# A new order table for a fused attention and adapter kernel on one core

## The chip, the core and the metric

The kernel runs on one NeuronCore of a Trainium2 chip. TensorE (PE) does the matmuls and their weight loads, VectorE (DVE) and ScalarE (ACT) turn what stands in PSUM into bf16 tiles in SBUF, GpSimd (POOL) only issues loads, and SyncE (SP) issues stores and transposing transfers. The metric is device microseconds of one launch. A span runs from the first to the last instruction of one profiled execution.

## The reference

Relu-squared attention over 8 batches of 12 heads, 448 positions and 64 columns, and after it a mixture of two out of eight rank-16 adapters on the 3584 x 768 result:

```python
def _attn_ref(q, k, v):
    scores = q.shape[-1] ** -0.5 * np.matmul(q, k.transpose(0, 1, 3, 2))
    attn = np.maximum(scores, 0.0) ** 2 / S
    return np.matmul(attn, v)

def _moe_ref(x, w_gate, A, B):
    logits = x @ w_gate
    topk = np.argpartition(-logits, 2, axis=1)[:, :2]
    w = softmax(logits at topk)
    ...
    delta[mask] += w[mask, k, None] * ((x[mask] @ A[e]) @ B[e])
    return x + delta
```

## The kernel before

`build` makes a list of some 1,100 operations, each a short run of instructions for one engine, and `ordered` puts them in the order of the string `ORDER`, which also gives each its PSUM banks (`@4`) and, where two engines can do it, its engine (`:A` for ACT, `:D` for DVE). Nothing else orders the work: each engine runs its instructions strictly in the order of the table and waits on semaphores for what an instruction reads or overwrites. The durations that operations carry (`act`, `dve`, 0.81 and so on) are for a planner outside and do not run on the chip.

A tile is one of 24 pairs (b, q) of batch and quad of four heads. Its names are:

- `f` with a number: operations without a key, above all the loads of q, k and v, two DMAs each, from POOL (`load`, L185). Buffers: five q, five k, eight v. They are named `q_5_1` for tile (5, 1). `f24` is the load of B (L248).
- `tp`, `te`: transposes of q and k on PE (L313), and their copy to the tile `qT` on DVE (L327, L335).
- `qk` n, `relu` n, `sq` n, `pv` n: for n from 0 to 173, one block of scores on PE (four 64x64 matmuls, L452), its relu out of PSUM on ACT (L472) or DVE (L474) into the tile `a`, the square of two or three blocks on DVE (L489), and the product with v (L520). There are eleven `a` buffers. A number of `relu` is used as a clock in what follows: "at relu 100" means where that word stands in the table.
- `x`: the result of seven `pv`, cast into `xt` by ACT or DVE (L565).
- `z`, `gmax` to `gzp`, `zt`, `zT`: gate and adapter input of a group of three 128-row tiles: PE (L582), small DVE and ACT steps, PE transposes (L644), and the copy `zT` by ACT or DVE (L661).
- `b`, `o`, `st`: half an output tile on PE, three transposes of `xt` (L728) and an fp32 product with B in two passes (L737); its copy out of PSUM by ACT or DVE (L773) or, for tiles 15 to 23, its sum with a transposed `xt` on DVE (L764); the store from SP or ACT (L783). For tiles 15 to 23 `xb` are transposing DMAs on SP (L677).
- `f86` is a run of eight matmuls on zeros (L348); `f84`, `f85`, `f87` are the first transposes and `f88` to `f91` their copies.

The gate's product leaves, per row, 128 adapter columns and then 8 logits, side by side in PSUM; `aw` builds the weights for that (L258).

Of the kernel before, what the change touches and what calls it, by code (L numbers as in the profile page):

```python
# [14 lines left out]
J = 7  # L15
CUT = 3
SPIN = 8
PH = 64
QUADS = 3
NB = 8  # L20
S = J * PH
# [12 lines left out]
C = dict(late=6, xi=(), om=(), merge_x=0, sqp=((999, (2, 2, 3)),), om2=(), fl=(), gf=(), ai=4, tg=((15, 3), (18, 3), (21, 3)), sp=(), xbdur=1.45, bx=8, xh=2, apart=3, apcap=1, gl=(3, 1), tqlat=2.0)  # L34
# [5 lines left out]
f4 f3 f1 f0 f2 f6 f5 f8 f7 f11 f9 f10 f84@0 f12 f88 f85@2 f90 f89 f13 f87@4 qk0@6 f91 qk1@0 relu0:D qk2@2 f14  # L40
relu1:A qk3@4 relu2:D relu3:A tp2@6 f17 qk4@0 te2 relu4:A qk5@2 qk6@4 sq2 tp3@6 f16 relu5:A f86@0 te3 relu6:A
sq0 qk7@0 f15 qk8@2 qk9@6 relu7:A tp4@4 relu8:D relu9:A f18 qk10@0 te4 qk11@2 relu10:A qk12@6 sq4 tp5@4 f19
relu11:A qk13@0 relu12:A te5 tp6@2 f26 sq9 relu13:A qk14@4 qk15@6 tp7 relu14:A f23 sq7 pv0@0 pv1 pv2 relu15:A
pv3 qk16@4 te6 pv4 pv5 f20 relu16:A pv6 qk17@6 x13:D pv7@2 relu17:A qk18@4 sq11 f22 pv8 pv9 x12:A qk19@6
relu18:A pv10 qk20@0 relu19:D f21 pv11 relu20:A pv12 pv13 qk21@4 sq16 x27:A qk22@6 f27 qk23@0 relu21:A aw1@3
sq14 relu22:A f33 x26:D relu23:A qk24@4 tp8@6 ae1 f25 relu24:A sq18 qk25@0 qk26@2 tp9 relu25:A f55 pv14@4 pv15
pv16 te8 relu26:A pv17 qk27@0 f31 pv18 pv19 relu27:A pv20 sq23 qk28@2 qk29@6 x41:A f28 qk30@0 x40:D relu28:A
aw0@5 sq25 relu29:A f29 relu30:A qk31@2 ae0 tp10@6 tp11 f32 relu31:A sq21 qk32@4 qk33@0 relu32:A te10 pv21@2 f30
pv22 pv23 relu33:A qk34@4 sq30 qk35@6 relu34:A qk36@0 f37 relu35:D relu36:A qk37@4 pv24 pv25 relu37:A pv26 sq32
f35 qk38@6 tp12@0 pv27 relu38:A tp13 qk39@4 f43 x55:A te12 qk40@6 x54:A z0@3 relu39:A sq35 qk41@0 f34 z1  # L50
relu40:A qk42@4 relu41:D z2 relu42:A f38 qk43@6 gmax0 tp14@0 relu43:A sq28 qk44@4 tp15 f42 relu44:A gd0 qk45@6
gu0 te14 relu45:A qk46@4 f50 gt0 sq39 qk47@0 relu46:A pv28@6 pv29 pv30 gsg0 pv31 f24 relu47:A qk48@4 pv32 gw0
pv33 sq44 f48 pv34 relu48:A qk49@0 gzp0 x69:A f36 tp18@4 sq37 relu49:A tp19 pv35@2 zt0@7 zt1 zt2 x68:A f41 te18
qk50@0 zT0:A pv36 pv37 relu50:A qk51@6 sq46 pv38 pv39 f47 relu51:A pv40 qk52@4 qk53@0 pv41 relu52:A x82:D tp16@6
tp17 relu53:A te16 qk54@4 b2@2 relu54:A f44 sq49 qk55@0 o2:A qk56@6 qk57@4 relu55:A relu56:D b0@2 f49 x83:A
relu57:D qk58@0 o0:A qk59@6 f39 relu58:A z3@3 z4 sq51 relu59:A qk60@4 qk61@0 z5 f40 sq56 relu60:A b4@2 relu61:A
gmax3 qk62@6 f46 sq58 b1@4 relu62:A gu3 gd3 qk63@0 o4:A gt3 f65 sq42 qk64@6 gsg3 o1:A b3@5 relu63:A gw3 gzp3
b5@2 f51 relu64:A sq60 zt3@4 zt4 o3:A zt5 pv42@0 o5:A pv43 st2 qk65@6 zT3:A sq53 pv44 pv45 relu65:A qk66@2 st4
pv46 pv47 pv48 relu66:A tp20@4 st0 qk67@6 x96:D tp21 x97:A te20 f53 pv49@2 relu67:A pv50 qk68@0 pv51 pv52 sq63
relu68:A pv53 f66 pv54 pv55 qk69@4 qk70@6 x110:A relu69:D qk71@0 relu70:A f45 b6@2 x111:D relu71:A qk72@4 o6:D  # L60
tp22@6 relu72:A sq65 qk73@0 tp23 pv56@2 relu73:A pv57 f74 qk74@4 te22 pv58 pv59 relu74:A pv60 qk75@0 f79 pv61
sq67 pv62 relu75:A qk76@6 b8@4 f64 relu76:A x124:D qk77@0 x125:A sq70 tp24@6 relu77:A tp25 qk78@2 f59 z6@5 te24
relu78:A qk79@0 z7 relu79:A f52 o8:D qk80@2 qk81@6 sq72 z8 relu80:A b10@4 f54 gmax6 relu81:A sq77 qk82@0 tp26@2
# [81 lines left out]
def build(k=None, c=C):  # L145
# [31 lines left out]
    def load(b, w, q, deps):  # L177
        nm = "qkv"[w]

        def fn():  # L180
# [7 lines left out]
        o = op(("POOL",), 1.17, fn, deps=deps, kind="load", take=(nm, "lane"), give=("lane",))  # L188
        o.mb = 1.35
        return o  # L190

# [763 lines left out]
```

## Time and profile before

| | us |
|---|---|
| median of 3 runs (181.57 to 182.73) | 181.69 |
| span of the profiled execution | 179.6 |
| PE busy | 165.1 |
| DVE busy | 163.5 |
| ACT busy | 156.2 |
| POOL busy | 90.7 |

The profiled execution's own time is not recorded beside its span; the median run stands 2.1 us above the span. An engine's busy time is the union of its instructions' spans, and instructions that follow each other on one engine overlap in these spans by some 0.1 to 0.2 us, so the pace of an engine is read from start to start, not from the mean duration. A busy PE is not PE at its peak.

In a timeline each row is: start, duration, engine, line, operation, output <- input, how many instructions are merged, and in brackets the idle time before and what ended it. In a table of stretches each row is: from and to, length, busy time of PE, PEld (weight loads), DVE, ACT and POOL with instruction counts, the granted clock as a share of 2.4 GHz, the DMA share and GB/s.

### The profile page before, as it was taken

How to read it: one execution, taken by the hardware profiler on the slowest of the kernel's cores; microseconds unless marked ns; L12 is line 12 of the kernel's file. 1: busy time of each engine (PE TensorE's matmuls, PEld its weight loads, DVE VectorE, ACT ScalarE, POOL GpSimd, SP SyncE). 2: the span in 40 equal slices, each digit the busy share in tenths (PEclk: the TensorE clock that was granted, in tenths of full speed). 3: DMA queues.
4: the chain of work that ended last, by engine and by line, in shares of the span. 5: the costliest groups of instructions: out<-in, count | busy, mean ns of one | idle time of the engine just before them, and what ended most of it. 6: DMA issues, size and time to landing. Idle time of an engine off the chain costs nothing.

```text
span 179.6 us, 7694 instructions
## 1 busy us (share of the span) xinstructions
PE 165.1 (92%) x3366; PEld 99.2 (55%) x3366; DVE 163.5 (91%) x254; ACT 156.2 (87%) x240; POOL 90.7 (50%) x155
## 2 busy tenths in 40 slices
PE   7887998888899999999979899999999999999990
PEld 2445476454535665646646465655666557576650
DVE  0699999999989999999999899999999999999831
ACT  3399999999999999999998999999999899993120
POOL 7999997988869377850966867250000000000000
PEclk9999999999999999999999999999999999999999
DMA  4999999999999999994699999988495663515644
GB/s 90 126 170 188 164 112 183 164 180 178 202 180 152 186 303 166 175 166 130 84 176 299 197 185 268 237 118 222 113 171 149 45 223 63 189 42 211 230 194 158
DMA packets 33985, 30.49 MB, mean 170 GB/s; under 512 B 11488, under 2 KB 30432, under 8 KB 33952
## 3 DMA queue, kind: packets, MB, share of 16 engines
q0 software_dynamic: 22000, 17.03, 65.7%
q1 hardware_dynamic: 11376, 11.90, 22.1%
q10 hardware_dynamic: 576, 1.08, 1.6%
q8 instruction: 26, 0.43, 0.9%
q14 instruction: 7, 0.06, 0.1%
HBM read 33.84 MB, written 11.01 MB: 250 GB/s over the span
## 4 chain that ended last, share of the span: by engine, by line
PE 44%; ACT 16%; DMA 16%; POOL 15%; issue 4%; DVE 2%; ACTq 0%; POOLq 0%
PE ps L737 17%; ACT a L472 14%; DMA q<-in_q_dram 9%; PE ps L452 9%; PE ps L520 8%; POOL k L185 5%; PE ps L582 4%; POOL v L185 4%; DMA B<-in_moe_B_dram 4%; POOL q L185 3%; PE ps L728 3%; DMA k<-in_k_dram 3%; PE ps L313 2%; ACT osb L773 2%; PE ps L644 1%
## 5 line engine op out<-in xcount | busy, mean ns | idle before, releaser
L472 ACT ACTIVATE a<-ps 128x896 bf16<-128x896 f32 (+3 forms) x158 | 132.7, 961 | 3.3 <-PE ps L452 3.0
L489 DVE TENSOR_TENSOR a<-a 128x1792 bf16<-128x1792 bf16 (+4 forms) x75 | 88.5, 1193 | 0.0
L452 PE MATMUL ps<-qT 64*64 64x448 bf16 (+2 forms) x756 | 57.9, 345 | 4.5 <-ACT a L472 3.3
L737 PE MATMUL ps<-B,zT 128*128 128x384 f32 x112 | 47.5, 514 | 0.3 <-DMA B<-in_moe_B_dram 0.3
L520 PE MATMUL ps<-a,v 64*64 64x448 bf16 (+2 forms) x756 | 44.3, 330 | 0.8 <-ACT a L472 0.4
L452 PEld LDWEIGHTS <-qT 64*64 64x64 bf16 x756 | 25.3, 106 | 31.9 <-issue 22.9
L185 POOL DMA_DIRECT2D k<-in_k_dram x46 | 27.8, 629 | 16.3 <-PE ps L452 7.1
L185 POOL DMA_DIRECT2D v<-in_v_dram x48 | 28.8, 621 | 8.1 <-PE ps L452 3.8
L185 POOL DMA_DIRECT2D q<-in_q_dram x48 | 29.4, 639 | 3.5 <-DMA v<-in_v_dram 1.5
L520 PEld LDWEIGHTS <-v 64*64 64x64 bf16 x756 | 22.6, 106 | 7.9 <-issue 2.7
L327 DVE COPY qT<-ps 128x1792 bf16<-128x1792 bf16 x21 | 22.8, 1084 | 0.7 <-ACT a L472 0.4
L565 ACT CAST xt<-ps 128x448 bf16<-128x448 f32 (+2 forms) x37 | 19.4, 560 | 2.6 <-PE ps L520 2.3
L773 ACT COPY osb<-ps 128x384 f32<-128x384 f32 x26 | 13.1, 529 | 7.4 <-PE ps L737 5.6
L737 PEld LDWEIGHTS ps<-B,zT 128*128 128x128 f32 x112 | 17.3, 190 | 3.7 <-DMA B<-in_moe_B_dram 0.4
L474 DVE TENSOR_SCALAR a<-ps 128x896 bf16<-128x896 f32 (+1 forms) x16 | 16.9, 1069 | 0.9 <-PE ps L452 0.9
L313 PEld LDWEIGHTS <-q 64*64 64x64 bf16 x672 | 10.4, 112 | 6.9 <-issue 3.3
L582 PEld LDWEIGHTS <-xt 128*128 128x128 bf16 x168 | 10.5, 98 | 5.7 <-issue 4.7
L582 PE MATMUL ps<-awg,xt 128*128 128x136 bf16 x168 | 13.5, 223 | 0.0
L728 PEld LDWEIGHTS <-xt 128*128 128x128 bf16 x114 | 8.0, 98 | 9.9 <-issue 8.1
L313 PE MATMUL ps<-identb,q 64*64 64x64 bf16 x672 | 10.9, 197 | 2.3 <-DMA q<-in_q_dram 1.1
L728 PE MATMUL ps<-identb,xt 128*128 128x128 bf16 x114 | 12.7, 220 | 0.2
L565 DVE CAST xt<-ps 128x448 bf16<-128x448 f32 (+2 forms) x17 | 9.6, 570 | 0.2 <-PE ps L520 0.2
(47 smaller groups left out, 97.9 us busy)
## 6 DMA issues: line engine op xcount, KB each, us to landing
out_dram<-osb SPq DMA_DIRECT2D x25, 384.0 KB, 4.2
q<-in_q_dram POOLq DMA_DIRECT2D x48, 112.0 KB, 5.0
v<-in_v_dram POOLq DMA_DIRECT2D x48, 112.0 KB, 4.9
k<-in_k_dram POOLq DMA_DIRECT2D x46, 112.0 KB, 4.9
out_dram<-osb ACTq DMA_DIRECT2D x2, 384.0 KB, 2.3
B<-in_moe_B_dram POOLq DMA_DIRECT2D x1, 384.0 KB, 6.6
xb<-xt SPq DMA_TRANSPOSE x18, 3.2
a_raw<-in_moe_A_dram POOLq DMA_DIRECT2D x1, 192.0 KB, 5.4
```

Of the source, the lines that this page charges most:

```text
L185: nc.gpsimd.dma_start(out=t[g * PH : g * PH + PH], in_=k.qkv[w][b, g, :, 2 * q : 2 * q + 2, :])
L313: nc.tensor.transpose(k.ps_b[sl * PH : sl * PH + PH, o.banks[g], (w * J + j) * PH : (w * J + j) * PH + PH], source(w, j)[r, sl], k.identb[ ...
L327: nc.vector.tensor_copy(t.rearrange("p g w x -> p g (w x)"), k.ps_b[:, m.banks[0] : m.banks[0] + 2, : 2 * S])
L452: nc.tensor.matmul(out=bank(o, sl)[g * PH : g * PH + PH, at : at + w].rearrange("k (j p) -> k j p", j=J), lhsT=t[r, g, 1, j * PH : j * PH ...
L472: nc.scalar.activation(out, flat(qk_ops[n], w), ACTF.Relu, scale=k.relu_scale)
L474: nc.vector.tensor_scalar(out, flat(qk_ops[n], w), k.relu_scale, 0.0, op0=ALU.mult, op1=ALU.max)
L489: nc.vector.tensor_mul(a, a, a)
L520: nc.tensor.matmul(out=bank(head, g)[sl * PH : sl * PH + PH, :w], lhsT=vn[r, sl, j * PH : j * PH + PH], rhs=T["a", g0][r, x + sl * width(n ...
L565: evac(w, lambda cp, g=g: cp(k.xt[:, g * QUADS + q, b * S + x0 : b * S + x1].rearrange("d (p j) -> d p j", j=J), bank(src, g)[:, :w].rearr ...
L582: nc.tensor.matmul(out=bank(zops[0])[:, t * ZW : t * ZW + ZW], lhsT=k.xt[:, do, 128 * tiles[t] : 128 * tiles[t] + 128], rhs=k.awg[:, do, : ...
L728: nc.tensor.matmul(out=out(h)[:, x * 128 : x * 128 + 128], lhsT=k.xt[:, 3 * h + x, c0 : c0 + 128], rhs=k.identb, start=(x == 0), stop=Fals ...
L737: nc.tensor.matmul(out=o, lhsT=T["zT", g0][:, zi], rhs=rhs, start=xb is not None, stop=True, skip_group_check=True,)
```

## The change

`ORDER` is replaced by another order of the same operations: the same 174 `qk`, 56 `b`, 72 loads and so on, with other places, PSUM banks and engines. Options of the planner that were unused are removed with their code, and the planner's durations are set anew. One layout changes with it: the gate's logit of an expert now stands behind that expert's 16 adapter columns instead of behind all 128, so the DVE steps read with a stride of 17. Matmul counts and shapes stay.

```diff
-C = dict(late=6, xi=(), om=(), merge_x=0, sqp=((999, (2, 2, 3)),), om2=(), fl=(), gf=(), ai=4, tg=((15, 3), (18, 3), (21, 3)), sp=(), xbdur=1.45, bx=8, xh=2, apart=3, apcap=1, gl=(3, 1), tqlat=2.0)
+C = dict(late=6, sq=((999, (2, 2, 3)),), merge_x=(), two=(), groups=(3, 3, 3, 3, 3, 3, 3, 3, 3, 1), ai=4, tg=((15, 3), (18, 3), (21, 3)))
...
-f4 f3 f1 f0 f2 f6 f5 f8 f7 f11 f9 f10 f84@0 f12 f88 f85@2 f90 f89 f13 f87@4 qk0@6 f91 qk1@0 relu0:D qk2@2 f14
...
+f6 f3 f8 f4 f0 f1 f7 f2 f9 f11 f10 f12 f84@0 f85@2 f13 f88 f89 f5 f90 f86@4 qk0@2 f87@4 f91 f14 f16 qk1@0 f17 qk2@6
+relu0:A qk3@4 relu1:A qk4@2 relu2:D sq0 relu3:A qk5@0 relu4:A tp2@6 tp3@4 qk6@2 te2 relu5:A te3 qk7@4 relu6:A tp4@0
...
-                    for rhs, lo, hi in ((k.a_raw[:, :, i, :], 0, RE), (k.g_raw[:, i, :], RE, ZW)):
+                    for rhs, lo, hi in ((k.a_raw[:, :, i, :], 0, R), (k.g_raw[:, i, :, None], R, R + 1)):
                         nc.tensor.matmul(
-                            out=bank(m)[:, x * ZW + lo : x * ZW + hi],
+                            out=bank(m)[:, x * ZW : x * ZW + ZW].rearrange("p (e s) -> p e s", e=E)[:, :, lo:hi],
...
-                nc.vector.max(mx[:, t, :], z3()[:, t, RE:ZW])
+                nc.vector.max(mx[:, t, :], zv()[:, t // m, t % m, :, R])
...
             nc.vector.tensor_tensor(
-                new("zp", ("zp", g0), [128, 3, E, R], F32)[:, :n],
-                z3()[:, :, 0:RE].rearrange("p t (e r) -> p t e r", e=E),
-                T["wt", g0][:, :n, :, None].to_broadcast([128, n, E, R]), op=ALU.mult)
+                z.rearrange("p (a t) (e r) -> p a (t e) r", a=A, e=E),
+                zv().rearrange("p a t e s -> p a (t e) s")[:, :, :, :R],
+                w[:, :, :, None].to_broadcast([128, A, m * E, R]), op=ALU.mult)
```

Three places of the new table, by engine. The first is the start of DVE's row, from the last copy into the first tile's `qT`. `a_0` holds blocks 0 and 1, `a_2` blocks 2 and 3. Before:

```order
L335 COPY qT_0_0_152<-ps_94 128x2x256
L474 TENSOR_SCALAR a_0_212<-ps_94 128x896
L474 TENSOR_SCALAR a_2_226<-ps_94 128x896
L335 COPY qT_0_1_264<-ps_94 128x2x448
L489 TENSOR_TENSOR a_2_226<-a_2_226 128x1792
L335 COPY qT_0_1_264<-ps_94 128x2x448
L489 TENSOR_TENSOR a_0_212<-a_0_212 128x1792
```

The same place on DVE now:

```order
L334 COPY qT_0_0_182<-ps_94 128x2x256
L410 TENSOR_SCALAR a_2_244<-ps_94 128x896
L425 TENSOR_TENSOR a_0_233<-a_0_233 128x1792
L334 COPY qT_0_1_314<-ps_94 128x2x448 x2
L425 TENSOR_TENSOR a_2_244<-a_2_244 128x1792
L334 COPY qT_0_2_358<-ps_94 128x2x448
L410 TENSOR_SCALAR a_7_352<-ps_94 128x896
```

`relu0` has left DVE for ACT, and on PE `qk0` has moved ahead of the last transposes (`f87`) that the first row's copy waits for.

The second place is POOL's row around the load of B. Before:

```order
L185 DMA q_3_2_1048<-in_q_dram 64x2x448 x2
L185 DMA q_2_2_1072<-in_q_dram 64x2x448 x2
L185 DMA k_3_0_1095<-in_k_dram 64x2x448 x2
L185 DMA v_2_2_1168<-in_v_dram 64x2x448 x2
L185 DMA k_4_1_1188<-in_k_dram 64x2x448 x2
L248 DMA B_97<-in_moe_B_dram 128x768
L185 DMA v_3_1_1235<-in_v_dram 64x2x448 x2
```

And now:

```order
L184 DMA q_3_0_629<-in_q_dram 64x2x448 x2
L184 DMA k_3_0_632<-in_k_dram 64x2x448 x2
L184 DMA q_2_1_648<-in_q_dram 64x2x448 x2
L184 DMA k_2_1_653<-in_k_dram 64x2x448 x2
L184 DMA v_1_1_665<-in_v_dram 64x2x448 x2
L247 DMA B_97<-in_moe_B_dram 128x768
L184 DMA v_1_2_687<-in_v_dram 64x2x448 x2
```

B's load has moved up past seven rows of POOL: it stands at row 36 of that engine, where it stood at row 43.

The third place is POOL's row around the q of tile (5, 1). Before:

```order
L185 DMA k_5_0_2098<-in_k_dram 64x2x448 x2
L185 DMA q_6_2_2114<-in_q_dram 64x2x448 x2
L185 DMA k_7_2_2257<-in_k_dram 64x2x448 x2
L185 DMA v_4_2_2289<-in_v_dram 64x2x448 x2
L185 DMA q_5_1_2315<-in_q_dram 64x2x448 x2
L185 DMA k_7_1_2392<-in_k_dram 64x2x448 x2
```

And now:

```order
L184 DMA q_5_0_2241<-in_q_dram 64x2x448 x2
L184 DMA k_7_0_2272<-in_k_dram 64x2x448 x2
L184 DMA v_4_2_2346<-in_v_dram 64x2x448 x2
L184 DMA v_4_1_2436<-in_v_dram 64x2x448 x2
L184 DMA q_5_1_2454<-in_q_dram 64x2x448 x2
L184 DMA v_6_1_2457<-in_v_dram 64x2x448 x2
```

The load `k_7_2` no longer stands ahead of `q_5_1`; it has moved to a later place on POOL.

## Rows read from the trace of the kernel before

**Rows 1.** The page: busy by engine, and the clock in 40 slices.
```profile
PE 165.1 (92%) x3366; PEld 99.2 (55%) x3366; DVE 163.5 (91%) x254; ACT 156.2 (87%) x240; POOL 90.7 (50%) x155
...
PEclk9999999999999999999999999999999999999999
```
**Rows 2.** Stretches of ten microseconds.
```profile
110.00:120.00 10.00, 10.00 (x126) 5.64 (x129) 9.73 (x19) 9.88 (x16) 4.82 (x9) 1.00 1.05 185
...
140.00:150.00 10.00, 9.99 (x179) 5.89 (x175) 9.90 (x22) 9.11 (x17) 0.00 (x0) 1.00 0.45 126
...
160.00:170.00 10.00, 10.00 (x159) 6.90 (x148) 9.27 (x28) 3.85 (x10) 0.00 (x0) 1.00 0.46 177
```
**Rows 3.** Timeline of ACT, a run of nine relus and what follows it.
```profile
29.42 7.67 ACT L472 ACTIVATE a<-ps 128x896 bf16<-128x896 f32 x9
36.92 1.03 ACT L565 CAST xt<-ps 128x448 bf16<-128x448 f32 x2
```
**Rows 4.** Timeline of the start, all engines.
```profile
5.91 0.53 ACT L335 COPY qT<-ps 128x448 bf16<-128x448 bf16 x1 [2.90 <-PE ps L313]
6.31 0.13 PEld L313 LDWEIGHTS <-k_rest 64*64 64x64 bf16 x2 [0.57 <-DMA k_rest<-in_k_dram]
...
6.81 1.73 PE L452 MATMUL ps<-qT 64*64 64x448 bf16 x16
...
7.46 2.09 DVE L474 TENSOR_SCALAR a<-ps 128x896 bf16<-128x896 f32 x2
...
7.83 6.83 ACT L472 ACTIVATE a<-ps 128x896 bf16<-128x896 f32 x8 [1.38 <-PE ps L452]
```
**Rows 5.** Timeline around the first output tile, all engines.
```profile
44.23 0.64 POOL L248 DMA_DIRECT2D B<-in_moe_B_dram  x1
...
50.83 0.91 PE L737 MATMUL ps<-B,zT 128*128 128x384 f32 x2 [0.27 <-DMA B<-in_moe_B_dram]
...
51.78 0.48 ACT L773 COPY osb<-ps 128x384 f32<-128x384 f32 x1 [0.31 <-PE ps L737]
52.16 0.92 ACT L472 ACTIVATE a<-ps 128x896 bf16<-128x896 f32 x1
```
**Rows 6.** Timeline around the transposes of tile (5, 1): POOL, PE, ACT.
```profile
85.61 1.20 POOL L185 DMA_DIRECT2D k<-in_k_dram  x2 [6.06 <-PE ps L452]
...
87.94 1.24 POOL L185 DMA_DIRECT2D q<-in_q_dram  x2
...
93.87 0.41 PE L313 MATMUL ps<-identb,q 64*64 64x64 bf16 x26 [0.91 <-DMA q<-in_q_dram]
...
94.51 0.92 ACT L472 ACTIVATE a<-ps 128x896 bf16<-128x896 f32 x1 [0.52 <-PE ps L452]
...
95.70 0.48 ACT L773 COPY osb<-ps 128x384 f32<-128x384 f32 x1 [0.27 <-PE ps L737]
```
**Rows 7.** Timeline of PE, outputs among score and value blocks.
```profile
108.41 0.33 PE L728 MATMUL ps<-identb,xt 128*128 128x128 bf16 x3
...
109.27 0.33 PE L728 MATMUL ps<-identb,xt 128*128 128x128 bf16 x3
...
110.23 0.76 PE L452 MATMUL ps<-qT 64*64 64x448 bf16 x12
...
115.22 1.12 PE L520 MATMUL ps<-a,v 64*64 64x448 bf16 x20
116.17 0.36 PE L452 MATMUL ps<-qT 64*64 64x448 bf16 x4
```
**Rows 8.** Timeline of PE near the end.
```profile
160.89 2.82 PE L737 MATMUL ps<-B,zT 128*128 128x384 f32 x8
...
166.71 0.49 PE L644 MATMUL ps<-identf,zp 128*128 128x128 f32 x3
```
**Rows 9.** Stretches of two microseconds, early.
```profile
12.00:14.00 2.00, 1.42 (x52) 0.73 (x41) 2.00 (x3) 2.00 (x4) 1.60 (x4) 1.00 1.21 188
14.00:16.00 2.00, 1.47 (x68) 0.90 (x63) 2.00 (x3) 2.00 (x3) 2.00 (x4) 1.00 1.23 195
```

More of the change, by code (lines that the diff above doesn't have):

```diff
@@ L17 @@
 SPIN = 8
+APART = 3
 PH = 64
+GM = 4
 QUADS = 3
@@ L186, in fn @@
                                     in_=k.qkv[w][b, g, :, 2 * q : 2 * q + 2, :])
[L188 removed]
+        o = op(("POOL",), 1.17, fn, deps=deps, kind="load", take=((nm, (b, q)),))
         o.mb = 1.35
@@ L377, in tp @@
         return [[e]] * J
-    def turn_qk(b, q):
-        def dup():
-            t = T["whole", "k", b, q]
-            nc.vector.tensor_copy(t[:, 2 * S :], t[:, :PH])
-        def turn(x):
-            if ("qT", b, q) not in T:
-                new("qT", ("qT", b, q), [128, 3, J, 128], BF16)
-            t = T["whole", "kq"[x == 0], b, q]
-            at = PH * (x == 2)
-            nc.sync.dma_start_transpose(out=T["qT", b, q][:, x], in_=t[:, at : at + 2 * S])
-        d = op(DVE, 0.1, dup, deps=[loaded[b, 1, q]], key=("dup", 3 * b + q))
-        ts = []
-        for x in range(3):
-            ts.append(op(("SP",), c["xbdur"], lambda x=x: turn(x), kind="turn", key=("qt", 9 * b + 3 * q + x),
-                         deps=[loaded[b, 0, q] if x == 0 else loaded[b, 1, q] if x == 1 else d],
-                         after=ts[-1] if ts else None, take=() if ts else ("qT",), give=("q",) if x == 0 else ("k",) if x == 2 else (), lat=c["tqlat"], to=more))
-            ts[-1].mb = 1.1
-        return [ts] * J
@@ L476, in relu @@
         o = op(ANY, {"ACT": act(2 * w) + 0.005, "DVE": dve(2 * w)}, fn, deps=[qk_ops[n]],
-               after=relu_ops.get(n - 1), kind="relu", key=("relu", n), take=("a",) if i == 0 else (),
+               after=relu_ops.get(n - 1), kind="relu", key=("relu", n), take=(("a", g0),) if i == 0 else (),
                free=[(qk_ops[n], None)])
@@ L537, in pv @@
         return o
-    def idle(n, head, after):
-        def fn():
-            for g in range(2):
-                r = slice(g * PH, g * PH + PH)
-                for sl in range(2):
-                    nc.tensor.matmul(
-                        bank(head, g)[sl * PH : sl * PH + PH, :S], lhsT=k.zeros[r, :PH], rhs=k.zeros[r, :S],
-                        start=False, stop=False,
-                    )
-        return op(PE, S / 2400 + 0.01, fn, after=after, mode="64", kind="spin", ni=8, key=("fl", n))
     def xt_copy(n):
@@ L721, in osb, with out @@
             return T["osb", tl]
+        def out(h):
+            return bank(obs[0], h) if two else bank(obs[h])
         for h in range(2):
-            xb = xb_of.get((tl, h)) if xi is None else None
+            xb = xb_of.get((tl, h))
             def f_b(h=h, xb=xb):
-                for x in range(0 if xb or xi else 3):
+                for x in range(0 if xb else 3):
                     nc.tensor.matmul(
```

337 lines of the change are left out of this document (120 added, 217 removed).

## The prediction

> **What bounds the kernel now.** I read the page first. PE, DVE and ACT are each busy for 156 to 165 of 179.6 us, and the clock is full in every slice [rows 1]. No engine is idle for another to be made faster, so a new order can only win back waits. The stretches of ten microseconds say where such waits are: from 110 on PE is busy throughout, with DVE and ACT within 0.3 us of it at first, then ACT falls to 9.11 in 140 to 150 and, once the last relu is done, to 3.85 in 160 to 170 [rows 2]. The reader is to see two regimes: up to about 100 us the two engines that empty PSUM set the pace, later PE does, and the end is PE's outputs alone. What is worth something is a wait of two engines at once, and the timeline shows three before 100 us: the start [rows 4], the first output [rows 5], and the transposes of tile (5, 1) [rows 6].
>
> The pace comes from starts: nine relus of 448-wide blocks run from 29.42 to 36.92, 0.83 us each [rows 3]. A copy of half an output tile takes ACT 0.38 (51.78 to 52.16) [rows 5]. A `pv` or `qk` takes PE 0.19: five of them, 20 matmuls, from 115.22 to 116.17 [rows 7].
>
> **The change part by part.** *The start.* ACT's first relu begins at 7.83, DVE's at 7.46, although the last copy that `qk0` needs, on ACT, ends at 6.44 (5.91 and 0.53) [rows 4]. Before, PE goes to the remaining transposes first, which wait for their DMA until 6.31, and starts `qk0` at 6.81; its relu follows 0.65 later. Now `qk0` stands ahead of these transposes and `relu0` is ACT's. It can start at about 6.5 and its relu at about 7.2. The zeros run `f86` now lies between 5.9 and 6.5, where PE waited anyway. ACT so begins 0.6 earlier. The bounds are 0, if the zeros delay `qk0` by as much, and 0.9, the full distance from 6.9. I take 0.6, the lag that the first row shows.
>
> *The load of B.* Its DMA is issued at 44.23 and PE waits for it at 50.83, by 0.27; ACT then waits 0.31 [rows 5]. In the new table the load stands seven POOL rows earlier, ahead of relu 24 instead of relu 47, and the first output that needs it only moves from relu 54 to relu 52. 23 places of 0.83 us against a shift of two leave no wait: 0.3 gained. Nothing is late in its stead on PE that the rows show.
>
> *The q of tile (5, 1).* POOL issues in order. `k_7_2`, which nobody needs for long, waits 6.06 us for a buffer until 85.61, and behind it `q_5_1` goes out at 87.94 and lands when PE has waited 0.91, at 93.87; ACT loses 0.52 and 0.27 behind that [rows 6]. Counted in the table with five buffers of q, each load taking the one freed longest ago, the last release that `q_5_1` or a load ahead of it waits for is at relu 89 before and its transposes at relu 100: 11 relus, 9 us, and from 85.61 to 93.87 the load takes 8.3. Now that release is at relu 82 by the same count and the transposes are at relu 103: 21 relus, 17 us. For all q and k loads behind the start the shortest distance is now 13 relus, where four loads had 11 or 12. I take the whole 0.9; the bounds are 0 (another late load) and 0.9.
>
> *Changes of shape on PE.* Between work in 64x64 quarters and work on the full array PE loses time: an output half after another starts 0.86 later (108.41 to 109.27), but a score block after an output half 0.96 later (109.27 to 110.23), so one change costs 0.1 [rows 7]. The old table has 99, the new one 91. Only those behind relu 100, where PE is the bound, are paid: 54 against 52, 0.2 gained. The other six lie under ACT; if they counted as well the gain would be 0.8.
>
> *Who copies.* Up to the last relu ACT has one relu less, three `zT` more and one output copy more: -0.83 + 4 x 0.38 = +0.7. DVE sheds the like; a relu there takes about 1.0 (2.09 for two) [rows 4] and a copy not less than ACT's 0.38, so it changes by 1.0 - 4 x 0.38 = -0.5 or more. Three further output copies move to ACT in the tail, where ACT is idle [rows 2]: nothing. With both engines about as busy I put the shift at 0, between -0.5 and +0.7.
>
> *The tail.* After the last `qk` the new table still has the three `zt` of tiles 21 to 23 ahead of the rest of PE's outputs; all else there is the same work, eleven output halves behind the last `pv` in both. Three `zt` take at most 0.49, 0.3 from start to start, and one change 0.1 [rows 8, 7]: 0.4 lost, with nothing to hide it since PE has no gaps there [rows 2].
>
> *The strided gate.* The DVE steps read the same elements with another stride. No row shows a strided read of this kind; ten small groups lie under DVE's queue. Taken as 0, with bounds of 0 and 0.5.
>
> *The sparse start of PE.* Between relu 7 and relu 22 the old table has 14 `pv`, the new one none; they come in relus 23 to 30. PE's work there falls by 14 x 0.19 = 2.7 us. It costs nothing if PE's clock holds: the old run's sparsest stretches, 1.42 and 1.47 busy of 2.00, show a granted clock of 1.00, which is the 2.4 GHz level [rows 9]. The Trainium skill, "TensorE: Matmul & The Clock Gate", Part 1, says the opposite of harmless: half clock is the default and only activity releases it. By that rule the sum would lose time here; no row before shows a fall, and I keep it as a rival.
>
> Sum: -0.6 - 0.3 - 0.9 - 0.2 + 0 + 0.4 + 0 = -1.6 us. The span of 179.6 becomes 178.0. The profiled execution's own time is not recorded; the median of 181.69 stands 2.1 above the span, so I predict 180.1.
>
> **The rivals.** *More comes back.* ACT's missing 0.89 in 140 to 150 [rows 2] is PE arriving late, and if the new table has PE less loaded there, that goes too, and with it the other six changes of shape (0.6) and 0.5 from DVE's lighter share: 180.1 - 0.89 - 0.6 - 0.5 = 178.1. For it speaks that at relu 150 PE has less behind it; against it that the same work is paid later.
>
> *PE runs dry, then is overfull.* Behind relu 150 the new table keeps three output halves more (2.82 for four [rows 8], 0.7 each), four `pv` more (0.19) and two changes fewer: 2.1 + 0.8 - 0.2 = 2.7 us more of PE work, in the part where PE is the bound. Before relu 150 PE is relieved by the same, which helps only if ACT and DVE run faster for it. If half is lost, 180.1 + 1.3 = 181.4; if all, 182.8.
>
> *The clock falls.* This one makes it slower. If PE's granted clock drops to the 1.2 GHz level between relu 7 and 22 and is still there when `pv0` starts, the stretch from relu 20 to 30 has 22 blocks, 22 x 0.19 = 4.2 us at full clock and 8.4 at half, against ten relus of 0.83; the transposes and the placing of the weights there no longer fit beside ACT. I price it with one doubling of the blocks, 4.2: 184.3. It decides from the point where the clock is still half at `pv0`; if it falls and is back by then, it is free, since 15 relus take 12 us and PE's blocks there 2.9, or 5.7 at half. The skill's page above is the rule behind it.
>
> **How the numbers follow.** About 1% (1.8 us) can be told from no change here: faster is below 179.9, slower above 183.5. The forecast gets 0.46, with 179.0 to 181.2 as its own range, of which 0.18 lies below the line; the rich case 0.24, the overfull PE 0.18, the clock 0.12. Faster: 0.18 + 0.24 = 0.42. Within: 0.28 + 0.18 = 0.46. Slower: 0.12. The range goes from 177.6, a little below the rich case, to 183.0, just above all of the overfull PE; it leaves out the clock case and the far end of the rich one.
>
> **What would show it.** In the new profile: ACT's first relu at about 7.2; no wait of PE for B or for a q load in the middle; PE's last `qk` about 2 us earlier, and from there to the end 0.4 us more than now; the clock full in every slice. A PE that is idle around relu 140 to 150 and then busy to the end without ACT at its side would show the overfull case; a clock digit of 5 near 15 to 25 us the slow one. The prediction is wrong if waits of a new kind, between PE and the engines that empty PSUM, take the place of the three named: rows of the old run cannot show those.

## The result: 1.2% slower, and the profile after

| | before | after |
|---|---|---|
| median of 20 runs each, us | 181.6 (180.35 to 183.39) | 183.75 (182.21 to 186.43) |
| ratio, 95% interval | | 1.0124 (1.0102 to 1.0146) |
| time of the profiled execution, us | not recorded | 182.21 |
| its span, us | 179.6 | 180.2 |

All ratios leave disturbed runs out, and each is to runs of the kernel before on the same chip. The predicted 180.1 and its range, 177.6 to 183.0, are missed on the slow side. The profiled execution is the fastest of the 20; a second profile stands under the experiments.

The page of the kernel after, busy time by engine and the clock in 40 slices, answers to [rows 1]:

```profile
PE 165.1 (92%) x3366; PEld 99.8 (55%) x3366; DVE 160.6 (89%) x247; ACT 158.2 (88%) x247; POOL 91.0 (50%) x155
...
PEclk9999789999999999999999999999999999999999
```

PE is busy for as long as before, ACT for 2.0 us more and DVE for 2.9 less; the span is 0.6 us longer because the engines wait elsewhere. The stretches of ten microseconds, as in [rows 2]:

```profile
10.00:20.00 10.00, 6.48 (x227) 3.37 (x216) 10.00 (x12) 10.00 (x14) 9.21 (x16) 1.00 1.21 180
20.00:30.00 10.00, 9.64 (x252) 6.81 (x254) 10.00 (x11) 9.90 (x14) 9.93 (x16) 0.83 1.11 141
...
90.00:100.00 10.00, 9.78 (x218) 5.49 (x204) 9.91 (x16) 10.00 (x18) 7.73 (x13) 1.00 0.96 154
...
140.00:150.00 10.00, 10.00 (x171) 6.18 (x168) 9.47 (x14) 9.42 (x18) 0.00 (x0) 1.00 0.40 100
150.00:160.00 10.00, 8.80 (x192) 5.67 (x188) 8.36 (x19) 7.50 (x15) 0.00 (x0) 1.00 0.74 188
160.00:170.00 10.00, 10.00 (x148) 6.87 (x141) 8.54 (x22) 4.11 (x11) 0.00 (x0) 1.00 0.33 122
```

The reader is to see a hole in all three engines at once in 150 to 160, where the kernel before has this:

```profile
150.00:160.00 10.00, 10.00 (x211) 6.46 (x207) 9.89 (x21) 9.49 (x19) 0.00 (x0) 1.00 0.44 121
```

The timeline shows what the hole is (SP issues the transposing transfers `xb` on L577 and the stores on L656; L643 is DVE's sum, L388 a score block, L408 a relu on ACT):

```profile
131.56 15.89 SPq L577 DMA_TRANSPOSE xb<-xt  x11
...
147.56 3.25 SPq L656 DMA_DIRECT2D out_dram<-osb  x3
...
150.86 2.81 SPq L577 DMA_TRANSPOSE xb<-xt  x2
...
155.94 1.02 DVE L643 TENSOR_TENSOR osb<-ps,xb 128x384 f32<-128x384 f32 x2 [1.60 <-DMA xb<-xt]
...
156.55 0.57 PE L388 MATMUL ps<-qT 64*64 64x126 bf16 x26 [1.20 <-DVE osb L643]
...
157.00 1.70 ACT L408 ACTIVATE a<-ps 128x1008 bf16<-128x1008 f32 x2 [1.21 <-DVE osb L643]
```

In the new table the transfer `xb113` is the first of the two at 150.86, behind the stores `st30`, `st34`, `st32`; the sum `o41` needs it at 154.3 and gets it at 155.94. The 3.25 us of the three stores are not 3.25 us of work. SP is done with `st30` at 148.08 and then stands at `st34`, which stores the sum that DVE makes at 149.42:

```profile
149.42 0.55 DVE L643 TENSOR_TENSOR osb<-ps,xb 128x384 f32<-128x384 f32 x1
...
150.00 0.81 SPq L656 DMA_DIRECT2D out_dram<-osb  x2
```

So `xb113` goes out late because it stands behind a store that waits for its data, and it then takes 4.96 us to land.

The start, against [rows 4]:

```profile
5.82 0.58 PE L312 MATMUL ps<-identb,q 64*64 64x64 bf16 x26 [0.47 <-DMA q<-in_q_dram]
...
6.16 1.09 PE L347 MATMUL ps<-zeros 64*64 64x512 bf16 x8
...
7.00 0.63 PE L388 MATMUL ps<-qT 64*64 64x448 bf16 x4
...
7.67 2.54 ACT L408 ACTIVATE a<-ps 128x896 bf16<-128x896 f32 x3 [0.69 <-PE ps L388]
```

In this execution ACT's first relu begins 0.16 earlier than before, not 0.6, since half of the first q landed later; the zeros cost nothing, as `qk0` starts at 7.00 and ACT's copy for it ends at 6.98. The waits for B and for `q_5_1` of [rows 5, 6] are gone; in the list of PE's waits the only one for a q load is the one at the start:

```profile
PE ps L312 <- DMA q<-in_q_dram: 0.5, 1, 0.5
```

**One way to read all profiles.** Let A be the start of ACT's first relu of a 322-wide block, which is `relu147` in both orders, and Z the end of the last score block; both are rows of the timeline.

| profile of | A | Z | A to Z | Z to end of span |
|---|---|---|---|---|
| before | 140.28 | 160.24 | 19.96 | 19.4 |
| before, thin `pv` early | 139.09 | 159.05 | 19.96 | 19.4 |
| before, two loads moved | 139.68 | 159.64 | 19.96 | 19.4 |
| before, transposes ahead | 141.85 | 161.81 | 19.96 | 19.3 |
| after | 137.00 | 160.21 | 23.21 | 20.0 |
| after, second profile | 139.28 | 162.61 | 23.33 | 20.0 |
| after, `xb113` ahead of the stores | 137.35 | 159.01 | 21.66 | 20.0 |
| the same, second profile | 138.95 | 160.61 | 21.66 | 20.0 |
| after, stores on ACT | 138.55 | 160.62 | 22.07 | 19.5 |
| after, zeros early | 140.81 | 162.51 | 21.70 | 20.7 |
| after, zeros early and `xb113` ahead | 141.03 | 163.26 | 22.23 | 21.0 |

From A on the old order takes 39.3 us in each of its profiles, the new one 43.2 or 43.3 in its two, and 41.6 or 41.7 with `xb113` ahead. The two profiles with zeros are the exceptions: nothing is changed in them behind A but what their names say, and the first has no wait for `xb` although `xb113` stands behind the stores. There it goes out at 154.72, as long behind A as in the first profile after (13.9 us), but lands 3.39 us later and not 4.96. The 1.6 us are so a matter of a late issue and a slow landing together; two of three profiles have them.

So the new order loses 3.9 us behind A. An estimate for the usual execution: a median of 183.75 (about 181.7 of span) puts A at 138.5, and 181.6 (179.5) puts it at 140.2 before, which is 1.7 gained ahead of A and 2.2 lost in all, against 2.15 between the medians.

The gain ahead of A has one place. These rows begin with `relu100`, in the kernel after, before, and before with thin `pv` early:

```profile
91.75 1.16 ACT L408 ACTIVATE a<-ps 128x896 bf16<-128x896 f32 x1
```
```profile
91.87 0.93 ACT L472 ACTIVATE a<-ps 128x896 bf16<-128x896 f32 x1
```
```profile
91.69 0.92 ACT L472 ACTIVATE a<-ps 128x896 bf16<-128x896 f32 x1
```

From there to A the new order takes 45.2 us in every profile of it without zeros; the old one takes 48.4 with the wait for `q_5_1`, and 47.4 to 47.9 in its four other profiles. So the gain is about 2.2 us where that wait is absent, and 1.4 to 2.6 when it is counted from other relus between 40 and 110. It comes from PE work which the new table puts off, and A to Z is where that work comes back.

### The profile page after: what moved, and what is told of

Its sections match the earlier page's. It is cut to its first block, busy times and chain, and to the rows that moved or that the text cites. A ratio compares the mean times of both kernels' runs of the same rounds, so it can differ in the third digit from the quotient of the medians.

```text
span 180.2 us, 7694 instructions
## 1 busy us (share of the span) xinstructions
PE 165.1 (92%) x3366; PEld 99.8 (55%) x3366; DVE 160.6 (89%) x247; ACT 158.2 (88%) x247; POOL 91.0 (50%) x155
## 4 chain that ended last, share of the span: by engine, by line
PE 55%; ACT 20%; DVE 12%; DMA 5%; issue 5%; SPq 0%; POOL 0%; ACTq 0%; DVEq 0%; POOLq 0%
PE ps L619 18%; ACT a L408 16%; PE ps L388 12%; PE ps L443 11%; DVE a L425 5%; PE ps L490 4%; PE ps L614 4%; PE ps L312 4%; DVE a L410 3%; DMA xb<-xt 3%; ACT xt L472 2%; DMA q<-in_q_dram 2%; PE ps L554 1%; DVE qT L326 1%; DVE qT L334 1%
## 5 line engine op out<-in xcount | busy, mean ns | idle before, releaser
L408 ACT ACTIVATE a<-ps 128x896 bf16<-128x896 f32 (+3 forms) x157 | 136.7, 998 | 3.0 <-PE ps L388 1.4
L388 PE MATMUL ps<-qT 64*64 64x448 bf16 (+2 forms) x756 | 60.7, 349 | 7.4 <-ACT a L408 4.0
L388 PEld LDWEIGHTS <-qT 64*64 64x64 bf16 x756 | 25.8, 106 | 36.0 <-issue 27.2
L443 PEld LDWEIGHTS <-v 64*64 64x64 bf16 x756 | 23.1, 107 | 10.7 <-issue 5.1
L472 ACT CAST xt<-ps 128x448 bf16<-128x448 f32 (+2 forms) x38 | 20.3, 574 | 3.2 <-PE ps L443 3.1
L646 ACT COPY osb<-ps 128x384 f32<-128x384 f32 x30 | 17.8, 600 | 1.8 <-PE ps L619 1.8
L410 DVE TENSOR_SCALAR a<-ps 128x896 bf16<-128x896 f32 (+1 forms) x17 | 18.1, 1071 | 0.7 <-PE ps L388 0.5
L643 DVE TENSOR_TENSOR osb<-ps,xb 128x384 f32<-128x384 f32 x18 | 9.4, 551 | 1.9 <-DMA xb<-xt 1.6
L312 PE MATMUL ps<-identb,q 64*64 64x64 bf16 x672 | 10.4, 197 | 0.5 <-DMA q<-in_q_dram 0.5
```

What stands on the lines that cost most here:

```text
L312: nc.tensor.transpose(k.ps_b[sl * PH : sl * PH + PH, o.banks[g], (w * J + j) * PH : (w * J + j) * PH + PH], source(w, j)[r, sl], k.identb[ ...
L388: nc.tensor.matmul(out=bank(o, sl)[g * PH : g * PH + PH, at : at + w].rearrange("k (j p) -> k j p", j=J), lhsT=t[r, g, 1, j * PH : j * PH ...
L408: nc.scalar.activation(out, flat(qk_ops[n], w), ACTF.Relu, scale=k.relu_scale)
L410: nc.vector.tensor_scalar(out, flat(qk_ops[n], w), k.relu_scale, 0.0, op0=ALU.mult, op1=ALU.max)
L443: nc.tensor.matmul(out=bank(head, g)[sl * PH : sl * PH + PH, :w], lhsT=vn[r, sl, j * PH : j * PH + PH], rhs=T["a", g0][r, x + sl * width(n ...
L472: evac(w, lambda cp, g=g: cp(k.xt[:, g * QUADS + q, b * S + x0 : b * S + x1].rearrange("d (p j) -> d p j", j=J), bank(src, g)[:, :w].rearr ...
```

## The experiments

**The late transfer.** The kernel after with one word moved, in two runs on two chips:

```diff
-z23 st30 b40@4 relu164:A qk166@6 sq149 st34 st32 xb113 pv147@0
+z23 xb113 st30 b40@4 relu164:A qk166@6 sq149 st34 st32 pv147@0
```

> The new order with one move: the transposing transfer xb113 stands ahead of the stores st30, st34, st32 on SP instead of behind them. Late-transfer theory: the 1.6 us wait of DVE near 154 us (ACT and PE 1.2 behind it) goes and the kernel gets 1.2 to 1.6 us faster than the new order's 183.75; the mean granted clock stays near 0.97. Rival, that PE's backlog at the end covers that wait: under 0.5 us gained, PE as busy to the end.

> The changed kernel with xb113 ahead of the stores, unchanged from its first run, as the base of the three beside it: 181.2 to 182.0 us; from the first 322-wide relu to the end of the last score block 21.7 us as in its first profile.

Measured: 181.31 us, ratio 0.9996 (0.9973 to 1.0018), and 182.34, ratio 1.0033 (1.0002 to 1.0064). In the first profile SP takes the transfer in its row of transposes (twelve) and the stores come after:

```profile
131.91 17.52 SPq L577 DMA_TRANSPOSE xb<-xt  x12
...
149.53 1.65 SPq L656 DMA_DIRECT2D out_dram<-osb  x3
...
154.63 1.02 DVE L643 TENSOR_TENSOR osb<-ps,xb 128x384 f32<-128x384 f32 x2
```

No wait is left at the sum, and A to Z falls by 1.55. The medians are 2.4 and 1.4 under the 183.75 of the kernel after. On the chip of the second run the kernel after had a ratio of 1.0117 (below) and this one 1.0033, which is 1.5 us. Is it the place on SP, or that the transfer stands near its reader? The latter, in the kernel before:

```diff
-relu154:A xb113 ... relu163:A xb130 qk164@4
+relu154:A ... relu163:A xb130 xb113 qk164@4
```

> The kernel before with one word of its table moved: the transfer xb113 goes from relu 154 to relu 163, four relus ahead of the output copy o41 that reads it (o41 stands at relu 167); in the changed kernel it stands five relus ahead of o41. Theory of the late transfer: four relus take 3.3 us, the transfer took about 5 from issue to landing in the changed kernel, so DVE waits about 1.7 for it, ACT and PE behind DVE lose 1.2 or more, and the time rises from 181.4 to between 182.6 and 183.8. Rival, that the place of this transfer is not what costs in the changed kernel (its wait is made good in the tail): 181.4, no change.

Measured: 181.51, ratio 0.9999 (0.9969 to 1.0029); A to Z is 19.96. The expectation fell: four relus ahead of the reader are enough where no store that waits stands in front. (Its profiled execution took 183.44, a long one; A to Z is the same in it.) Then the stores, in the kernel after:

```diff
-STORES = {24: 'ACT', 26: 'ACT'}
+STORES = {15: 'ACT', 16: 'ACT', 17: 'ACT', 24: 'ACT', 26: 'ACT'}
```

with the words `st30`, `st34`, `st32` as `st31`, `st35`, `st33`, as the names go.

> The changed kernel with the order of its transfers as it is, but the three stores ahead of xb113 issued from ACT's queue, so that SP goes from its row of eleven transposing transfers straight to xb113. Theory that SP's queue makes it late: DVE's wait for xb goes from 1.60 to 0.3 or less, the stretch from 23.3 to 21.7 to 22.0, the time falls by 1.3 to 1.6 to that of the base. Rival, that the 1.2 MB of the three stores on the DMA engines make it late, wherever they are issued: the wait stays at 1 us or more and the time at 183 or more.

Measured: 181.25, ratio 0.9975 (0.9941 to 1.001). SP and DVE in that profile:

```profile
133.12 18.50 SPq L577 DMA_TRANSPOSE xb<-xt  x13
...
153.78 0.56 DVE L643 TENSOR_TENSOR osb<-ps,xb 128x384 f32<-128x384 f32 x1 [0.36 <-PE ps L388]
```

The wait for `xb` is gone, as the theory said: `xb113` goes out at 149.07 without waiting for a store. The rival is not ruled out by this, since ACT issues the three stores at 150.95 and later, behind the transfer; that their traffic slows a transfer issued beside them is not shown and not excluded. A to Z is 22.07, and Z to the end 19.5 instead of 20.0. The Trainium skill, "Perfetto Trace Analysis", DMA Optimizations, says that where the engine that issues DMAs is the bottleneck, balancing them over the engines that can issue may help; moving them did help here, 183.21 on this chip (next run) against 181.25, though SP was not busy but held up by a store.

**A second profile of the kernel after**, unchanged.

> The changed kernel as it is, on this chip, for a second profile: the first one was of an execution of 182.21 us, at the bottom of runs whose median is 183.75. Theory of the late transfer (the transposing transfer xb113 queued on SP behind three stores): 183 to 184.5 us, and a profile in which DVE's wait for xb is longer than the 1.60 of the first one, by about what this run is longer. Rival, the start: the extra time stands at 9 to 13 us, as a wait of PE for the second half of a k load like the 1.64 us in the profile with the zero matmuls, with the clock at its lower level around it, and the wait for xb is no longer than before. Rival, the clock: two stretches of the lower level instead of one, and ACT and DVE idle beside the second by 1 us or more.

Measured: 183.21 (182.44 to 184.83), ratio 1.0117 (1.0068 to 1.0167); the profiled execution took 184.49. The wait for `xb` is 1.59, so the first theory's longer wait is wrong; the extra 2.3 us is at the start, as the rival said:

```profile
10.72 0.41 PE L312 MATMUL ps<-identb,k 64*64 64x64 bf16 x26 [0.82 <-DMA k<-in_k_dram]
...
13.24 0.56 PE L312 MATMUL ps<-identb,q 64*64 64x64 bf16 x26 [0.90 <-DMA q<-in_q_dram]
...
14.59 10.83 ACT L408 ACTIVATE a<-ps 128x896 bf16<-128x896 f32 x13 [1.30 <-PE ps L388]
```

PE sits in transposes that wait for a load, and score blocks queue behind them. ACT's first relu stands at 7.09 in this profile, 0.74 earlier than before, and still the time is longer.

**What the stretch from A to Z is bound by.** All four start from the kernel with `xb113` ahead, and make three output halves thin: 64 of 384 columns.

```diff
+w_ = 64 if 2 * tl + h in (6, 8, 10) else W
-out=out(h)[:, :W], lhsT=..., rhs=k.B[:, h * W : h * W + W]
+out=out(h)[:, :w_], lhsT=..., rhs=k.B[:, h * W : h * W + w_]
```

> The changed kernel with xb113 ahead of the stores (181.31 us), in which three output halves that stand between relu 70 and relu 81 multiply 64 of 384 columns of B, so that part of three output tiles is left out. It takes about 3 x 0.58 = 1.7 us of work from PE there. Theory that ACT and DVE set the pace until about 110 us: 181.0 to 181.4, since PE is only waited for less. Rival, that PE's total work sets the time in this kernel: 179.6.

Measured: 182.04, ratio 1.0027 (0.9995 to 1.006), A to Z 21.66: no gain from PE work early (the base has 1.0033 on this chip). With (30, 32, 34):

> The same kernel as the one with the thin early halves, but the three halves (tiles 15 to 17, first half each) that stand behind relu 150 are the thin ones instead: the same 1.7 us of work taken from PE, in the part where the overfull-PE theory has it bound, and part of three output tiles is left out. Overfull PE (2.7 us more of PE work behind relu 150 than in the table before): the time falls by 1.4 to 1.8, to 179.5 to 179.9. Rival, that after relu 150 waits between PE and the engines that empty PSUM set the pace and not PE's amount of work: 181.0 to 181.4.

Measured: 181.55, ratio 1.001 (0.9983 to 1.0037); A to Z 21.48, 0.2 for 1.7 us of PE work. With (31, 35, 40):

> The changed kernel with xb113 ahead of the stores, in which three other output halves multiply 64 of 384 columns of B: those that stand at relu 158, 160 and 163, so that part of three output tiles is left out. The halves thinned in the run before lie at 140 to 145 us, where the chain of waits of that run still goes through DVE; from 144 on the chain of the unthinned kernel is PE alone up to the end. Theory that PE is overfull from 144 on: from the first product with v of 322-wide blocks to the last output matmul, 22.1 us in the unthinned kernel, 20.4 to 20.7 now, and the whole time 1.4 to 1.7 below the unthinned 181.3. Rival, that DVE's sums set the pace to the last score block as well: 22.0 and no change.

Measured: 181.22, ratio 0.9993 (0.9961 to 1.0026); A to Z 21.38, 0.3. PE's amount alone is not the bound, though PE is busy 6.00 of 6.00 there. (The 1.7 us are the estimate of the expectation, 3 x 0.58; PE's busy time from A to Z falls by 0.75, from 21.66 to 20.91.) The same halves thin in DVE's sum and in the store, not on PE:

> The base, in which the sums on DVE of the three output halves at relu 160, 162 and 167 (tiles 15, 17 and 20; their matmuls were the thin ones of the run before last) take 64 of 384 columns, and the stores of these tiles leave the other 320 out. About 3 x 0.4 = 1.2 us less for DVE, PE's work is whole. PE and DVE both full: as with PE alone thinned, the stretch from the first 322-wide relu to the end of the last score block falls by only 0 to 0.4, from 21.7 to between 21.3 and 21.7. Rival, DVE alone sets the pace there: 20.5 to 20.8, and the time 0.9 to 1.2 below the base.

Measured: 182.11, ratio 1.003 (0.9999 to 1.0061); A to Z 21.66, nothing. Both thin:

> The same three halves thin on both engines: 1.7 us less for PE and 1.2 for DVE. PE and DVE both full: the stretch falls by 0.9 to 1.5, to between 20.2 and 20.8, and the time by the same, which is what neither thinning alone brought. Rival, that a third thing (ACT, waits for PSUM banks) sets the pace: 21.3 or more, and no change.

Measured: 180.34, ratio 0.9942 (0.9907 to 0.9976), 2.0 below the base on its chip; but A to Z falls only by 0.65, to 21.01, between what was expected and what the rival said; how much of the rest is the start I can't tell. The stretch from 147 to 153 us shows why each falls short. PE, DVE and ACT are the first, third and fourth number after the length; the base, then PE thin, the sum thin, both thin:

```profile
147.00:153.00 6.00, 6.00 (x103) 4.04 (x102) 5.89 (x13) 5.62 (x11) 0.00 (x0) 1.00 0.59 194
```
```profile
147.00:153.00 6.00, 5.53 (x104) 4.05 (x103) 5.97 (x13) 6.00 (x13) 0.00 (x0) 1.00 0.60 200
```
```profile
147.00:153.00 6.00, 6.00 (x103) 3.98 (x101) 5.53 (x13) 5.62 (x11) 0.00 (x0) 1.00 0.58 177
```
```profile
147.00:153.00 6.00, 5.83 (x117) 4.28 (x104) 5.56 (x13) 6.00 (x12) 0.00 (x0) 1.00 0.53 164
```

Relieve PE and DVE is full at 5.97 and ACT at 6.00; relieve both and ACT is. Three engines are full within half a microsecond, so it is likely that work moved into this stretch costs, on whichever engine; no run moves it back. What was moved: PE's matmuls from the first 322-wide score block to Z, grouped by line, before and then in the new order (the kernel with `xb113` ahead):

```profile
L737 PE MATMUL ps<-B,zT 128*128 128x384 f32 x20 | 8.5, 525 | 0.0
...
L520 PE MATMUL ps<-a,v 64*64 64x322 bf16 (+1 forms) x112 | 5.7, 309 | 0.0
L582 PE MATMUL ps<-awg,xt 128*128 128x136 bf16 x27 | 2.4, 223 | 0.0
```
```profile
L619 PE MATMUL ps<-B,zT 128*128 128x384 f32 x24 | 9.8, 516 | 0.0
...
L443 PE MATMUL ps<-a,v 64*64 64x322 bf16 (+1 forms) x140 | 7.2, 318 | 0.0
L490 PE MATMUL ps<-awg,xt 128*128 128x136 bf16 x20 | 1.7, 223 | 0.0
```

Four output matmuls (two halves) and 28 value matmuls (seven `pv`) more, seven gate matmuls fewer: 1.3 + 1.5 - 0.7 = 2.1 us of busy time against the 1.7 us by which A to Z is longer.

**The clock.** Four zero matmuls ahead of each of `qk8` to `qk22` in the kernel after, then the same with `xb113` ahead:

```diff
+if 8 <= n <= 22:
+    ... nc.tensor.matmul(bank(o, sl)[..., :448], lhsT=k.zeros[..., :PH], rhs=k.zeros[..., :448], ...)
```

> The new order with four matmuls on zeros ahead of each of the score blocks 8 to 22 (0.19 us of PE each, 2.9 in all). Clock theory: the granted clock stays at 1.00 between 15 and 30 us, the mean is above 0.99, and the kernel gets about 1.6 us faster than 183.75, the distance between the profiled run (clock 0.991) and the median run (clock 0.972). Rival, that the low clock lies hidden under ACT: clock full, time unchanged within 0.5 us or longer by the added work.

> Both edits. If the late transfer and the clock are two separate costs, the gains add up: about 2.8 us, 180.9, 0.4% below the old order. If only one of them is on the path, it equals that one's run. If PE's added backlog behind relu 150 is the whole cause, neither helps and it stays above 183.

Measured: 184.72, ratio 1.0183 (1.0153 to 1.0212), and 186.43, ratio 1.0267 (1.023 to 1.0304). In the first the mean granted clock rises (0.988 to 0.995, where the kernel after has 0.965 to 0.991) and the time rises too; in the second it is 5 us above the same kernel without zeros. The zeros write the bank of the score block behind them, so they wait for the same relu and then stand in its way: 1.1 us of PE's waits for ACT are at the zeros. In the profile of the first, PE's wait for a k load, 1.64 at 11.64, comes ahead of the first zeros, and A is at 140.81. And the opposite, in the kernel before, 14 early `pv` thin, which leaves part of the output out:

```diff
+w_ = 64 if n < 14 else w
```

> The old order, in which the value products of the first two tiles (pv 0 to 13) use 64 of their 448 columns, so part of the output is left out: PE has 14 x 0.16 = 2.3 us less work between relu 14 and 23, the rest is as before. Clock theory: the granted clock falls near 20 us as in the new order, the mean goes below 0.99, and the time is the old one or up to 1.5 us longer although work was taken away. Rival, that the fall needs something else in the new order: clock 1.00, time within 0.3 us of the old one.

Measured: 181.96, ratio 1.0022 (0.9993 to 1.005); the profiled execution has a span of 178.4 although its clock is 0.64 in 20 to 22 and 0.50 in 22 to 24. In the kernel after the fall is this, in stretches of two microseconds:

```profile
18.00:20.00 2.00, 0.79 (x12) 0.25 (x12) 2.00 (x3) 2.00 (x4) 2.00 (x4) 1.00 1.20 175
20.00:22.00 2.00, 1.78 (x45) 1.01 (x48) 2.00 (x3) 2.00 (x3) 1.93 (x4) 0.52 1.49 171
22.00:24.00 2.00, 2.00 (x56) 1.45 (x52) 2.00 (x3) 1.98 (x3) 2.00 (x2) 0.63 1.24 158
24.00:26.00 2.00, 1.96 (x44) 1.39 (x34) 2.00 (x2) 1.93 (x3) 2.00 (x5) 1.00 0.67 82
```

The first products with v come inside the fall:

```profile
22.67 1.17 PE L443 MATMUL ps<-a,v 64*64 64x448 bf16 x12
```

PE does 0.79 of 2.00, then is granted the 1.2 GHz level for most of four microseconds; DVE stays full and ACT lacks 0.1, so it costs about that here. The Trainium skill, "TensorE: Matmul & The Clock Gate", Part 1, has half clock as the default that activity lifts; the trace agrees on the fall, and shows that what it costs hangs on whether another engine sets the pace then.

**The start and the loads.** In the kernel with `xb113` ahead, `tp3` goes back behind `qk6` and `tp4` behind `qk9`; in the kernel before, the reverse:

```diff
-relu4:A tp2@6 tp3@4 qk6@2 te2 ... relu6:A tp4@0 sq2 relu7:A qk8@6 te4 qk9@2
+relu4:A tp2@6 qk6@2 tp3@4 te2 ... relu6:A sq2 relu7:A qk8@6 qk9@2 tp4@0 te4
```

> The changed kernel with xb113 ahead of the stores, and the start partly put back: the transposes of the second tile's k (tp3) stand behind the last score block of the first tile, qk6, and those of the third tile's q (tp4) behind qk8 and qk9, as they stand in the table before. Theory that the start of the changed kernel is easily upset because PE sits in transposes that wait for a load while score blocks stand behind them (0.82 and 0.90 us in the second profile of the changed kernel, with 2.2 us lost up to 28 us): spans of 180.5 and more become rare, and the median falls to 180.9 to 181.3. Rival, that the loads are simply late in some executions and each order loses as much: the median stays between 181.3 and 182.

> The kernel before with the opposite of the start's repair: tp3 ahead of qk5 and qk6, and tp4 ahead of qk7 to qk9, as in the changed table. Theory that this is what makes the start easily upset: the median rises by 0.5 to 2 us, to 181.9 to 183.4, by executions that lose 2 us up to 28 us. Rival, that the place of these transposes doesn't matter: 181.4, with a spread like that of the kernel before.

Measured: 182.13, ratio 1.0048 (1.0022 to 1.0073), no repair; and 183.01, ratio 1.0097 (1.0063 to 1.013), so in the kernel before the place of these transposes is worth about 1.8 us. ACT and DVE there:

```profile
13.88 6.58 ACT L472 ACTIVATE a<-ps 128x896 bf16<-128x896 f32 x8 [1.06 <-PE ps L452]
...
14.33 1.09 DVE L474 TENSOR_SCALAR a<-ps 128x896 bf16<-128x896 f32 x1 [1.79 <-PE ps L452]
```

Three of its nine runs have a clock of 0.998 to 1.0 and still take 182.59 to 183.38: the waits cost by themselves. Last, in the kernel before only the two loads:

```diff
-qk41@0 f34 z1 ... pv31 f24 relu47:A ... relu90:A f80 qk91@6 ... x152:A f58 relu93:A
+qk41@0 f34 f24 z1 ... pv31 relu47:A ... relu90:A f58 f80 qk91@6 ... x152:A relu93:A
```

> The kernel before with the two loads alone: the load of B goes ahead of three rows of POOL (to relu 39), and the q of tile (5, 1) ahead of the k of tile (7, 2). The forecast put 0.3 and 0.9 us on them: 181.4 - 1.2 = 180.2, and no wait of PE for either load in the profile. Rival, that the two waits stand only in some executions of the kernel before (a profile of it with thin products early had neither, at a span of 178.4): the median falls by 0.3 to 0.6, to 180.8 to 181.1, and the fastest runs stay where they are, at 180.3 to 180.5.

Measured: 181.66, ratio 1.0022 (0.9987 to 1.0058). Not even the rival's 0.3 shows. The kernel before has these waits in some executions only: in the profile with thin `pv` PE does not wait for B, and at the transposes of `q_5_1` only the weight loads stop, for this long:

```profile
92.68 0.30 PEld L313 LDWEIGHTS <-q 64*64 64x64 bf16 x26 [0.17 <-DMA q<-in_q_dram]
```

No version that does all the work beat the kernel before beyond the interval; the one with the stores on ACT is level with it.

## Why the prediction was wrong, point by point

- **The step that failed** is the sum's view of what an order costs: it priced three waits at 0.6 + 0.3 + 0.9 = 1.8 gained and everything that the new order does to SP's queue at nothing. The runs show about the reverse: 1.6 lost at `xb113`, and of the three waits nothing gained by `relu100`, which starts at 91.8 to 94.1 in ten profiles with the new start and at 91.7 to 94.1 in four with the old.
- **The late transfer.** The 1.6 was no rival. The prediction walked POOL's queue for two loads and never SP's: three stores, one of them waiting for its sum, ahead of a transfer whose reader stands five relus on. "Waits of a new kind" was as near as it came. With the transfer elsewhere, or the stores on ACT, the ratio is 0.9996, 1.0033 or 0.9975: the loss is gone, and a gain is not there.
- **The start** was right at its first row and wrong in what follows from it. ACT's first relu stands at 6.75 to 8.09 in those ten profiles, at 7.2 or earlier in six, against 7.83 before. By `relu10` the lead is gone: 14.06 to 15.78, against 13.71 to 14.56 in the four. PE then waits for loads of the second tile, or ACT waits for PE behind them.
- **B and `q_5_1`**: the waits are gone, but the kernel before does not have them in every execution, and moving the two loads alone gained nothing. The forecast took the waits of one profile for those of the median.
- **PE runs dry, then is overfull.** I had counted 2.7 us more behind relu 150 and left it out of the sum as if it cost nothing. From A to Z it costs 1.7. But the other half of that rival, that PE's relief ahead helps only if ACT and DVE run faster for it, came out well: they do, by about 2.2 between `relu100` and A. Net the move costs nothing that these runs can tell, so the place of the times without the late transfer, 181.31 and 182.34, near the rival's 181.4 and 182.8, is luck. Its mechanism was too narrow as well: DVE and ACT are nearly as full as PE, so neither thinning PE nor thinning DVE shows it.
- **The tail** was right. PE's last output matmuls are these, before and after:

```profile
174.39 0.86 PE L737 MATMUL ps<-B,zT 128*128 128x384 f32 x2
```
```profile
174.76 0.86 PE L619 MATMUL ps<-B,zT 128*128 128x384 f32 x2
```

  They end 15.0 us behind Z before and 15.4 after: 0.4, as forecast. The other 0.2 from Z to the end lie behind PE's last matmul, in the last copy and store.
- **The clock** fell, which the forecast denied. The rival's condition was met too: the first product with v starts at 22.67, in the stretch at 0.63, before the clock is back. Its price of 4.2 was not paid, since the clock is at full again in 24 to 26 and ACT lacks only 0.1 in the fall. So the condition that the rival named does not decide, and the fall was nearly free. Longer falls in other executions come together with late loads, and how much of their time is theirs is not separated. The stretches that the prediction calls sparsest, 1.42 and 1.47 of 2.00, are not: 40 to 42 has 1.23, also at full clock.
- **Shapes, copies, the strided gate** were not measured by themselves; no wait in the profile points to them.

What stays open: what the usual execution of the new order loses ahead of `relu100`, about 0.4 us by the medians; why its loads at the start are late in some executions; and why the zeros cost more than they take, ahead of A and behind it. Putting the transposes back did not cure the first.

## What to carry to other kernels

A lead at a point in the middle is no gain until the work behind that point is counted on every engine: find a point after which an order takes the same time in most profiles, and compare orders on both sides of it. An early first instruction is no gain either, if the ones behind it wait for the next load. When a table is reordered, walk every queue, stores included: a transfer is as late as what stands ahead of it on its issuing engine, and a store there waits for its data. One profile is one execution; where a wait hangs on a load, a second profile tells whether the kernel has that wait or that execution had it.

## What the runs showed of the hardware

SP issues these transposing transfers one at a time, 1.4 us each in a row (eleven in 15.89). It takes its queue in order: from 148.08 to 150.00 it stood at a store whose sum was not done, with `xb113` behind. A transfer issued beside stores landed after 4.96 us (`xb113` in the first profile after) or 3.39 (with zeros early), one without a store just ahead of it after 2.34 (`xb113` moved ahead). A matmul engine shown 100% busy lost some 1.7 us of work (the estimate above) and gave back 0.2 to 0.3; the Trainium skill, "Perfetto Trace Analysis", Identifying the Most-Contended Engine, warns that PE's busy share is no measure of headroom, and the trace agrees, though DVE and ACT, nearly full there as well, would do as a reason too. Loads at the start landed at least 1.4 us apart in executions with the same start: the second k was there by 10.25 in the first profile after, and at 11.64 in the one with zeros, ahead of its first zeros.
